# Products of a linear-attention prologue on column halves and quarters of TensorE's array

## The chip, the cores and the metric

The kernel runs on one core of a Trainium2 chip. The metric is device time in microseconds of one execution, the median of several runs. The profile is of one execution of its own, with its own time.

## The reference

A linear attention with decay and bonus (4 batches, 8 heads, 768 tokens, 48 channels a head) feeds a mixture of 8 experts over 3072 tokens of 384 channels, whose gates are balanced by eight rounds of row and column scaling. All inputs are f32.

```python
for t in range(S):                                   # attention
    kt, vt, rt = k[:, :, t], v[:, :, t], r[:, :, t]
    cur = einsum('bhd,bhe->bhde', u[None] * kt, vt)
    y[:, :, t] = einsum('bhd,bhde->bhe', rt, state + cur)
    state = w[None, :, :, None] * state + einsum('bhd,bhe->bhde', kt, vt)
x = y.transpose(0, 2, 1, 3).reshape(B * S, H * D)    # experts
P = balanced(exp(x @ w_gate - max))                  # 8 rounds
for e in range(E):
    out += P[:, e:e+1] * (maximum(x @ w1[e], 0) @ w2[e])
```

## The kernel before, in words

The kernel has two parts that follow each other. The attention fills about the first 260 us; beside it the first expert (expert 0) is started. Then the other seven experts run as 14 half-expert stages, to the end. The change touches the attention alone.

The attention takes the tokens in 24 chunks of 128 (`tt`), six to a batch (`c = tt % 6`). Within a chunk the recurrence is written as products. The eight heads are handled as four pairs (`NPAIR`); each head's 48 channels are padded to 64 (`HP`), so that a pair fills the 128 partitions. The decay is folded into tables (`rtab`, `ktab`, `wbd`). All operands of these products are f32, and the trace shows each such product as two instructions on TensorE (two passes), each with a weight load of its own.

For each chunk there are these steps, each one a function:

- `prep` (line 488): r and k times their tables, `rp` on GpSimdE and `kp` on VectorE.
- `bonus_dot`, `bonus` (494, 503): the term with u, `rk`, mostly on GpSimdE.
- `stage_b` (513): `rp` and `kp` are transposed on TensorE (tiles `prT`, `pkT`); ScalarE copies them out to `rT`, `kT`.
- `stage_c` (524): the scores, `pA` (line 536): for each pair `a` and each head `g` of it, 64 partitions of `kT` are the weights (128 columns) and 64 of `rT` are streamed (128 columns). So two heads stand on the two row halves of the array at once. VectorE copies the scores through the causal mask into `at` (538). Unless it is the last chunk of a batch, the state follows: `pu` (546), for each pair `kp` (128 weight columns, two heads) times v of both heads (96 columns). Only the blocks that belong to one head are wanted, and the table `wbd`, which is zero elsewhere, clears the other blocks: `S = (pu + S) * wbd`, the sum on VectorE (556), the product on GpSimdE (557).
- `stage_d` (560), one chunk later: y in the bank `py`: for `c > 0` four products of `rT` with `S` (570; 128 weight columns, 96 streamed), then for each head `at` times v (573; 128 weight columns, 48 streamed). VectorE adds the bonus and takes the scale for the split.
- `scale_x`, `stage_e`, `stage_f` (583 to 613): x is scaled, transposed (`px`) and split into f16 high and low parts; the gate's logits are taken from them.

TensorE's instructions keep the order of the program, and so do all other engines' (class `InOrder`, line 21). The loop at 733 sets that order by hand: in step `i` it has `prep(i + 2)`, `stage_b(i + 1)`, `stage_c(i)`, `stage_e(i - 2)`, `stage_d(i - 1)` and `stage_f(i - 3)`, and between them `work(n)`, which issues whole units of expert 0 (tiles `ph`: 9 products of 384 columns; `po`: 12 of them). `prepare()` takes one step at a time of a list `side`: splitting expert 0's weights and building sums of tokens for the later experts, on VectorE, ScalarE and GpSimdE. `STEPS` (721) says how many of these steps come ahead of and behind `stage_d` in the first loop steps.

Of the kernel before, what the change touches and what calls it, by code (L numbers as in the profile page):

```python
# [8 lines left out]
F32 = mybir.dt.float32  # L9
# [3 lines left out]
ALU = mybir.AluOpType  # L13
# [19 lines left out]
def rwkv_sinkhorn_moe(  # L33
# [13 lines left out]
    V, S_, G, T, Q = (  # L47
        InOrder(tc, e) for e in (nc.vector, nc.scalar, nc.gpsimd, nc.tensor, nc.sync)
    )

    B, H, S, D = r.shape
    NT, DM = out.shape
    E, _, F = w1.shape
    P = 128
    C = 128
    NPAIR = H // 2
# [7 lines left out]
    HP = 64  # L64
# [63 lines left out]
    def pow2_scale(m, inv, s, down):  # L128
        V.tensor_scalar(inv, m, 1e-30, down, op0=ALU.max, op1=ALU.mult)
        V.tensor_single_scalar(  # L130
            inv.bitcast(I32), inv.bitcast(I32), EXP_MASK, op=ALU.bitwise_and
        )
        V.reciprocal(s, inv)
# [135 lines left out]
    ac = att.enter_context(tc.tile_pool(name="ac", bufs=1))  # L269
    ld = att.enter_context(tc.tile_pool(name="ld", bufs=3))  # L270
    at2 = att.enter_context(tc.tile_pool(name="at2", bufs=2))
    ps3 = att.enter_context(tc.tile_pool(name="ps3", bufs=4, space=PSUM))
# [69 lines left out]
    def fill(x_):  # L342
        n = x_.shape[1]
        S_.mul(
            x_.rearrange("p (a q) -> p a q", q=HP),
            unit[:, :1, 1:].broadcast_to([P, n // HP, HP]), 0.0,
        )
# [3 lines left out]
    wbd = ac.tile([P, NPAIR, 2, D], F32, name="wbd")  # L351
# [10 lines left out]
    rp_ = [ac.tile([P, H, HP], F32, name=f"rp{i}") for i in range(2)]  # L362
    kp_ = [ac.tile([P, H, HP], F32, name=f"kp{i}") for i in range(3)]
    at_ = [ac.tile([P, H, C], F32, name=f"at{i}") for i in range(2)]
    for t_ in rp_ + kp_:
        G.memset(t_[:, :, D:], 0.0)
    fill(at_[0].rearrange("p h c -> p (h c)"))

    rk0 = at2.tile([P, H, D], F32, tag="rk", name="rk_0", bufs=3)
# [91 lines left out]
    for j in range(2):  # L461
        rows = slice(j * HP, j * HP + D)
# [61 lines left out]
    def stage_c(tt):  # L524
        d = st[tt]
        c = tt % NCHB
        rT, kT = d["rT"], d["kT"]
        at = at_[tt % 2].rearrange("p (a g) c -> p g a c", g=2)
        pas = []
        for g in range(2):  # L530
            pa = ps3.tile([P, NPAIR, C], F32, tag="pa", name=f"pA_{tt}_{g}")
            pas.append(pa)
        for a in range(NPAIR):
            for g in range(2):
                rows = slice(g * HP, g * HP + HP)
                T.matmul(pas[g][:, a, :], kT[rows, a, :], rT[rows, a, :], start=True, stop=True)
        for g in range(2):
            V.copy_predicated(
                at[:, g], maski.unsqueeze(1).broadcast_to([P, NPAIR, C]), pas[g]
            )  # L540
        if c < NCHB - 1:
            vn = loads[tt]["v"]
            kp = kp_[tt % 3].rearrange("p (a j) d -> p a (j d)", j=2)
            pu = ps3.tile([P, NPAIR, 2 * D], F32, tag="pa", name=f"pu_{tt}")
            for p_ in range(NPAIR):
                T.matmul(
                    pu[:, p_, :], kp[:, p_, :],
                    vn[:, 2 * p_ : 2 * p_ + 2, :].rearrange("p j d -> p (j d)"),
                    start=True, stop=True,
                )  # L550
            sn = at2.tile([P, NPAIR, 2 * D], F32, tag="S", name=f"S_{tt}", bufs=3)
            wb = wbd.rearrange("p a j d -> p a (j d)")
            if c == 0:
                V.tensor_tensor(sn, pu, wb, op=ALU.mult)
            else:
                V.tensor_tensor(sn, pu, d["S"], op=ALU.add)
                G.tensor_tensor(sn, sn, wb, op=ALU.mult)
            st.setdefault(("S", tt + 1), sn)

    def stage_d(tt):  # L560
        d = st[tt]
        c = tt % NCHB
        vn = loads[tt]["v"]
        at = at_[tt % 2]
        py = ps3.tile([P, H, D], F32, tag="pa", name=f"py_{tt}")
        pyp = py.rearrange("p (a j) d -> p a (j d)", j=2)
        first = True
        if c > 0:
            for p_ in range(NPAIR):
                T.matmul(pyp[:, p_, :], d["rT"][:, p_, :], d["S"][:, p_, :], start=first, stop=False)  # L570
                first = False
        for h in range(H):
            T.matmul(py[:, h, :], at[:, h, :], vn[:, h, :], start=first, stop=(h == H - 1))
            first = False
        x = at2.tile([P, DM], F32, tag="x", name=f"x_{tt}")
        V.tensor_tensor(x, py.rearrange("p h d -> p (h d)"), d["av"].rearrange("p h d -> p (h d)"), op=ALU.add)
        m = at2.tile([P, 1], F32, tag="xm", name=f"xm_{tt}")
        V.tensor_reduce(m, x, axis=AX.X, op=ALU.max, apply_absolute_value=True)
        s = at2.tile([P, 1], F32, tag="xs", name=f"xs_{tt}")
        pow2_scale(m, inv_s[:, tt : tt + 1], s, 0.125)  # L580
        d["x"], d["s"] = x, s
# [134 lines left out]
    for sg in range(3):  # L716
# [2 lines left out]
        side += steps  # L719

    STEPS = {
        0: (2, 1), 1: (1, 2), 2: (3, 1), 3: (1, 1),
        4: (1, 1), 5: (1, 1), 6: (2, 1), 7: (1, 1), 8: (1, 1),
    }

    def n_steps(i):
# [6 lines left out]
    for i in range(NTT + 3):  # L733
# [15 lines left out]
        if i < NTT:  # L749
            bonus(i)  # L750
            if ("S", i) in st:
                st[i]["S"] = st.pop(("S", i))
            stage_c(i)
# [17 lines left out]
        if 1 <= i <= NTT:  # L771
            stage_d(i - 1)
# [417 lines left out]
    for s in range(NS):  # L1190
        tasks = stage_tasks(s)
        for g in range(NG):
            for j in range(2):
                for n, nxt in enumerate(g1_slots(s, g, j)):
# [3 lines left out]
                    i = j * NPR + n  # L1198
# [37 lines left out]
```

## Time and profile before

| what | us |
|---|---|
| median of 3 runs (1562.79 to 1563.94) | 1563.07 |
| the profiled execution's own time | 1562.66 |
| its span in the profile | 1561.0 |
| TensorE busy | 1550.4 |
| VectorE busy | 1021.1 |
| ScalarE busy | 673.6 |
| GpSimdE busy | 581.8 |

The profile comes from the hardware's records of one execution. PE is TensorE's products, PEld its weight loads, DVE VectorE, ACT ScalarE, POOL GpSimdE, SP the queue that issues most DMAs. A group row has the engine, the operation, the tile written and those read, the shape, the count, then the busy time in us and the mean of one in ns, then the idle time of the engine ahead of it and who ended it. `64*128` ahead of the shapes of a product is rows times columns of the array that it uses. Products overlap in the pipeline, so the mean of one is its latency, and not the distance to the next; that is read from the chain of waits, which follows the work that ended last back from the end and gives for each piece its start, its length and its count. Line numbers are of little help, since a helper (line 29) issues nearly all instructions: one goes by tiles.

### The profile page before, as it was taken

To read this page: it belongs to the slowest core of one execution; us is meant where nothing else is said; L and a number is where in the kernel's file an instruction comes from. 1 tells how busy PE (TensorE), PEld (TensorE's weight loads), DVE (VectorE), ACT (ScalarE), POOL (GpSimd) and SP (SyncE) were. 2 spreads that over 40 slices of the span, in tenths; PEclk is the share of its full clock that TensorE was granted. 3 is DMA by queue.
4 is the path that set the end of the run, shared out by engine and by line. 5 is a ranking of instruction groups with operands and counts; after the bars stand their busy time and mean duration, and the time that the engine had idled before them with its cause. 6 is when DMAs were issued, how large, how long until landed. Compare 5 with 4: busy or idle time off the path is not lost.

```text
span 1561.0 us, 24064 instructions
## 1 busy us (share of the span) xinstructions
PE 1550.4 (99%) x9297; PEld 898.9 (58%) x9297; DVE 1021.1 (65%) x1694; ACT 673.6 (43%) x1192; POOL 581.8 (37%) x686
## 2 busy tenths in 40 slices
PE   8999999999999999999999999999999999999999
PEld 6878776655555555555555555555555555555555
DVE  8876674957666676666676666666666656656554
ACT  4334333534444354544444454544444444535320
POOL 7767764620012424243342424342423324242200
PEclk9999999999999999999999999999999999999999
DMA  9333311221215657576766676665555555556433
GB/s 198 68 87 81 80 51 42 93 79 45 97 60 105 76 86 115 84 127 89 128 87 119 85 127 90 95 96 68 86 57 99 58 94 61 96 59 97 56 91 132
DMA packets 167638, 138.26 MB, mean 89 GB/s; under 512 B 90337, under 2 KB 161762, under 8 KB 167522
## 3 DMA queue, kind: packets, MB, share of 16 engines
q0 software_dynamic: 44928, 61.36, 33.0%
q1 hardware_dynamic: 122384, 75.35, 17.2%
q8 instruction: 73, 1.20, 0.3%
q14 instruction: 43, 0.35, 0.1%
q10 hardware_dynamic: 210, 0.00, 0.0%
HBM read 55.39 MB, written 80.23 MB: 87 GB/s over the span
## 4 chain that ended last, share of the span: by engine, by line
PE 95%; DVE 3%; POOL 0%; issue 0%; ACT 0%; POOLq 0%; DVEq 0%; ACTq 0%
PE po L29 47%; PE bZ L29 11%; PE bY L29 11%; PE ph L29 5%; PE bA L29 5%; PE bB L29 5%; PE py L29 3%; PE bC L29 2%; PE pA L29 1%; PE pu L29 1%; PE px L29 1%; PE prT L29 1%; PE pkT L29 0%; DVE ws L29 0%; POOL rk L29 0%
## 5 line engine op out<-in xcount | busy, mean ns | idle before, releaser
L29 PE MATMUL po<-ws,hbx 128*128 128x384 f16 x3360 | 736.8, 326 | 0.0
L29 POOL DMA_DIRECT2D accd<-stg x288 | 249.7, 867 | 695.8 <-ACT stg L29 677.4
L29 PEld LDWEIGHTS <-hbx 128*128 128x128 f16 x3504 | 336.3, 98 | 292.4 <-issue 0.9
L29 PEld LDWEIGHTS <-ws 128*128 128x128 f16 x3096 | 302.5, 98 | 243.9 <-issue 1.4
L29 ACT ACTIVATE hbx<-tb 128x512 f16<-128x512 f32 x224 | 141.0, 630 | 450.4 <-DVE tb L29 450.4
L29 PE MATMUL po<-ws,hb 128*128 128x384 f16 x1248 | 323.0, 326 | 0.8 <-DVE ws L29 0.8
L29 DVE TENSOR_TENSOR tb<-bY,tb 128x512 f32<-128x512 f32 x168 | 116.2, 692 | 195.7 <-PE bY L29 195.5
L29 ACT ACTIVATE stg<-po,pe 128x384 f32<-128x384 f32 x312 | 179.1, 574 | 121.7 <-PE po L29 96.0
L29 PE MATMUL bZ<-xv,ws 128*128 128x512 f16 x840 | 227.0, 379 | 0.4 <-DVE tb L29 0.4
L29 PE MATMUL bY<-xv,ws 128*128 128x512 f16 x840 | 227.0, 379 | 0.0
L29 DVE TENSOR_TENSOR tb<-bZ,tb 128x512 f32<-128x512 f32 x168 | 115.6, 688 | 136.0 <-PE bZ L29 136.0
L29 PEld LDWEIGHTS <-hb 128*128 128x128 f16 x1248 | 121.8, 98 | 93.9 <-issue 1.0
L29 POOL TENSOR_TENSOR ucb<-rawb 128x256 f32<-128x256 f32 x84 | 76.2, 957 | 117.9 <-DMA rawb<-in_moe_w_dram 117.9
L29 DVE TENSOR_TENSOR tb<-bB,tb 128x512 f32<-128x512 f32 x112 | 77.5, 692 | 48.8 <-PE bB L29 46.9
L29 PE MATMUL ph<-hbx,ws 128*128 128x384 f16 x576 | 104.2, 326 | 0.5 <-DVE hb L29 0.5
L29 DVE SCALAR_TENSOR_TENSOR hb<-tb,hbx 128x512 f16<-128x512 f32 x112 | 77.3, 690 | 24.6 <-ACT hbx L29 19.5
L29 PE MATMUL bA<-xv,ws 128*128 128x512 f16 x336 | 90.8, 379 | 0.0
L29 PE MATMUL bB<-xv,ws 128*128 128x512 f16 x336 | 90.8, 379 | 0.0
L29 DVE SCALAR_TENSOR_TENSOR hbx<-tb,hbx 128x512 f16<-128x512 f32 x112 | 78.0, 696 | 14.7 <-ACT hbx L29 10.4
L29 DVE SCALAR_TENSOR_TENSOR hb<-ph,hb 128x384 f16<-128x384 f32 x64 | 35.4, 554 | 43.5 <-ACT hb L29 43.1
L29 ACT COPY tb<-bZ 128x512 f32<-128x512 f32 x56 | 32.7, 585 | 65.5 <-PE bZ L29 65.5
L29 ACT ACTIVATE hb<-ph 128x384 f16<-128x384 f32 x64 | 31.1, 487 | 62.5 <-PE ph L29 61.6
(168 smaller groups left out, 1608.0 us busy)
## 6 DMA issues: line engine op xcount, KB each, us to landing
accd<-stg POOLq DMA_DIRECT2D x288, 192.0 KB, 3.6
rawb<-in_moe_w_dram SPq DMA_DIRECT2D x28, 768.0 KB, 6.8
e0d<-stg SPq DMA_DIRECT2D x48, 192.0 KB, 1.9
hb<-e0d SPq DMA_DIRECT2D x48, 192.0 KB, 3.8
vn<-in_v_dram SPq DMA_DIRECT2D x24, 192.0 KB, 2.9
accd<-stg SPq DMA_DIRECT2D x24, 192.0 KB, 1.8
accd<-hb POOLq DMA_DIRECT2D x24, 192.0 KB, 4.8
rawb<-accd SPq DMA_DIRECT2D x24, 192.0 KB, 2.4
```

The costliest lines, as they stand in the source:

```text
L29: return lambda *a, **k: self.tc.keep_in_program_order(f(*a, **k))
```

## The change

Four things are edited, all in the attention. The state's tiles `S` become three fixed ones, and their blocks that belong to no head are set to zero once at the start. The scores are issued in column halves as well as row halves, so each product has 64 rows and 64 weight columns, and the streamed 128 columns stay. The state is taken head by head: 64 weight columns of `kp`, and the 48 columns of v of that head alone, written to the head's own half of the partitions; the update of `S` is done in two half-partition operations on VectorE and two on GpSimdE. The products of y are issued for the two halves of the tokens (64 weight columns each). Three entries of `STEPS` move a preparation step of loop step 1 to loop step 0 and put one more into loop step 6.

```diff
+    ss_ = [ac.tile([P, NPAIR, 2, D], F32, name=f"S{i}") for i in range(3)]
...
+    for t_ in ss_:
+        for j in range(2):
+            G.memset(t_[j * HP : (j + 1) * HP, :, 1 - j, :], 0.0)
...
-                T.matmul(pas[g][:, a, :], kT[rows, a, :], rT[rows, a, :], start=True, stop=True)
+                for hs in (slice(0, HP), slice(HP, C)):
+                    T.matmul(pas[g][hs, a, :], kT[rows, a, hs], rT[rows, a, :], start=True, stop=True)
...
-            pu = ps3.tile([P, NPAIR, 2 * D], F32, tag="pa", name=f"pu_{tt}")
+            pu = ps3.tile([P, NPAIR, D], F32, tag="pa", name=f"pu_{tt}")
             for p_ in range(NPAIR):
-                T.matmul(
-                    pu[:, p_, :], kp[:, p_, :],
-                    vn[:, 2 * p_ : 2 * p_ + 2, :].rearrange("p j d -> p (j d)"),
-                    start=True, stop=True,
-                )
...
+                for j in range(2):
+                    T.matmul(
+                        pu[j * HP : (j + 1) * HP, p_, :], kp[:, p_, j * HP : (j + 1) * HP],
+                        vn[:, 2 * p_ + j, :], start=True, stop=True,
+                    )
+            sn = ss_[tt % 3]
+            for j in range(2):
+                rows = slice(j * HP, (j + 1) * HP)
...
+                    V.tensor_tensor(sn[rows, :, j, :], pu[rows], d["S"][rows, :, j, :], op=ALU.add)
+            if c:
+                for j in range(2):
+                    rows = slice(j * HP, (j + 1) * HP)
+                    G.tensor_tensor(
+                        sn[rows, :, j, :], sn[rows, :, j, :], wbd[rows, :, j, :], op=ALU.mult
+                    )
...
-                T.matmul(pyp[:, p_, :], d["rT"][:, p_, :], d["S"][:, p_, :], start=first, stop=False)
+                for hs in halves:
+                    T.matmul(
+                        pyp[hs, p_, :], d["rT"][:, p_, hs], d["S"][:, p_].rearrange("p j d -> p (j d)"),
+                        start=first, stop=False, skip_group_check=True,
+                    )
...
-            T.matmul(py[:, h, :], at[:, h, :], vn[:, h, :], start=first, stop=(h == H - 1))
+            for hs in halves:
+                T.matmul(
+                    py[hs, h, :], at[:, h, hs], vn[:, h, :],
+                    start=first, stop=(h == H - 1), skip_group_check=True,
+                )
...
-        0: (2, 1), 1: (1, 2), 2: (3, 1), 3: (1, 1),
-        4: (1, 1), 5: (1, 1), 6: (2, 1), 7: (1, 1), 8: (1, 1),
+        0: (2, 2), 1: (0, 2), 2: (3, 1), 3: (1, 1),
+        4: (1, 1), 5: (1, 1), 6: (2, 2), 7: (1, 1), 8: (1, 1),
```

More of the change, by code (lines that the diff above doesn't have):

```diff
@@ L543, in stage_c @@
             kp = kp_[tt % 3].rearrange("p (a j) d -> p a (j d)", j=2)
-            pu = ps3.tile([P, NPAIR, 2 * D], F32, tag="pa", name=f"pu_{tt}")
+            pu = ps3.tile([P, NPAIR, D], F32, tag="pa", name=f"pu_{tt}")
             for p_ in range(NPAIR):
-                T.matmul(
-                    pu[:, p_, :], kp[:, p_, :],
-                    vn[:, 2 * p_ : 2 * p_ + 2, :].rearrange("p j d -> p (j d)"),
-                    start=True, stop=True,
-                )
[L551 to L557, printed above, removed]
+                for j in range(2):
[6 more added lines that the diff above has]
+                rows = slice(j * HP, (j + 1) * HP)
+                if c == 0:
+                    V.tensor_tensor(sn[rows, :, j, :], pu[rows], wbd[rows, :, j, :], op=ALU.mult)
+                else:
+                    V.tensor_tensor(sn[rows, :, j, :], pu[rows], d["S"][rows, :, j, :], op=ALU.add)
[5 more added lines that the diff above has]
+                    )
             st.setdefault(("S", tt + 1), sn)
@@ L566, in stage_d @@
         pyp = py.rearrange("p (a j) d -> p a (j d)", j=2)
+        halves = [slice(i * HP, (i + 1) * HP) for i in range(2)]
         first = True
```

## The prediction

> **What bounds the kernel now.** I read the page first, then the table of busy time by stretch, then the chain of waits inside the attention, then the groups of that stretch. The page:
>
> ```profile
> span 1561.0 us, 24064 instructions
> ...
> PE 1550.4 (99%) x9297; PEld 898.9 (58%) x9297; DVE 1021.1 (65%) x1694; ACT 673.6 (43%) x1192; POOL 581.8 (37%) x686
> ...
> PE 95%; DVE 3%; POOL 0%; issue 0%; ACT 0%; POOLq 0%; DVEq 0%; ACTq 0%
> ```
>
> TensorE is 99% busy and carries 95% of the chain. A busy share tells nothing of the pace of its instructions, though, and the change touches only the attention, in the first 260 us. The table by stretch (busy us and count of PE, weight load, DVE, ACT, POOL, then granted clock, DMA share, GB/s):
>
> ```profile
> 20.00:60.00 40.00, 38.17 (x344) 31.95 (x343) 36.76 (x74) 13.85 (x25) 32.88 (x31) 1.00 0.65 137
> 60.00:100.00 40.00, 39.21 (x348) 31.90 (x346) 31.25 (x65) 15.83 (x29) 23.39 (x24) 1.00 0.30 58
> 100.00:140.00 40.00, 40.00 (x341) 31.14 (x340) 25.91 (x55) 14.49 (x29) 31.45 (x36) 1.00 0.43 101
> ...
> 220.00:260.00 40.00, 39.58 (x333) 30.38 (x331) 24.35 (x51) 10.95 (x24) 22.48 (x28) 1.00 0.07 26
> ```
>
> Until 60 us VectorE is 92% busy (36.76 of 40). From 60 us on it has room (31.25, then 24 to 26 of 40) and TensorE has none. The chain of waits from 60 to 260 us says the same:
>
> ```profile
> by line: PE ph L29 23.4%; PE py L29 22.3%; PE po L29 21.1%; PE pA L29 9.8%; PE pu L29 8.0%; PE px L29 4.2%; PE prT L29 3.7%; PE pkT L29 3.3%; DVE ws L29 1.3%; DVE xm L29 0.6%; DVE x L29 0.6%; DVE inv_s L29 0.3%; ACT xsc L29 0.3%; DVE hb L29
> ```
>
> The products that the change edits, py (y), pA (scores) and pu (state), are 40% of a 200 us chain that is nearly all TensorE. So each is worth its own length there, and about nothing before 60 us. How long each is, from the chain in order of time (start, us):
>
> ```profile
> 204.90 1.72 PE py L29 x16
> 207.68 1.46 PE ph L29 x9
> 209.14 1.09 PE pA L29 x16
> 210.24 1.06 PE pu L29 x8
> 211.30 1.95 PE po L29 x12
> ...
> 215.04 2.61 PE py L29 x24
> ...
> 241.81 1.09 PE pA L29 x16
> 242.91 2.06 PE po L29 x12
> ```
>
> Three things are to be read here.
>
> Pace: py with 24 instructions takes 2.61 us and with 16 takes 1.72, so one takes 0.89/8 = 0.111 us. The 16 pA are eight pairs, one on each half of the rows; at 0.111 a pair they would need 0.89.
>
> Change of shape: pA takes 1.09, so going from the whole array to row halves cost 1.09 - 0.89 = 0.20 us. pu, eight at 0.111, takes 1.06: going back cost 0.17. po right after pA takes 2.06 where it elsewhere takes 1.95: into an f16 product the return cost 0.11.
>
> What sets the 0.111: not the streamed columns, since py with 96 and with 48 of them and pu with 96 have the same pace. It is the weight load of 128 f32 columns. The groups from 60 to 260 us:
>
> ```profile
> L29 PE MATMUL py<-vn,at 128*128 128x48 f32 x304 | 36.3, 273 | 0.0
> L29 PE MATMUL pA<-rT,kT 64*128 64x128 f32 x288 | 20.9, 285 | 0.0
> L29 PE MATMUL pu<-vn,kp 128*128 128x96 f32 x120 | 17.0, 284 | 0.0
> L29 PE MATMUL py<-S,rT 128*128 128x96 f32 x128 | 16.5, 272 | 0.0
> ...
> L29 PEld LDWEIGHTS py<-vn,at 128*128 128x128 f32 x304 | 35.5, 192 | 0.0
> L29 PEld LDWEIGHTS px<-ident,xsc 128*128 128x128 f32 x59 | 7.6, 141 | 2.4 <-ACT xsc L29 0.8
> L29 PEld LDWEIGHTS pmax_w<-ident,wma 128*1 128x1 f32 x1 | 0.1, 84 | 0.0
> ```
>
> Each f32 product is two instructions (two passes). In this stretch there are 288/16 = 18 score blocks, 120/8 = 15 pu, 304/16 = 19 y products, of which 128/8 = 16 have the 8 state instructions.
>
> **The change, part by part.** *The pace of a half.* py and pu become pairs of instructions with 64 weight columns each, side by side in the array. Nothing in this trace loads 64 f32 columns, or works on column halves. From above: the load gets no shorter than in proportion, 0.111/2 = 0.056 us; from below: in the transposes a load of 1 column takes 84 ns and one of 128 takes 141, so 64 columns fewer are at least 57 x 64/127 = 29 ns less, and the pace 0.083. I take 0.058 (half and 2 ns), since py's own row is the nearest: its load lasts 192 ns and is the thing repeated every 111. Two other limits stay clear of it or take over:
>
> ```profile
> 217.65 0.13 PE px L29 x6
> ...
> 281.20 0.34 PE pc L29 x2
> ```
>
> The first is chain time of six load-and-multiply pairs in f16, 22 ns each, so a pair of halves can be issued in about 50 ns, and the four quarters in about 100. The second streams 192 f32 columns twice in 0.34 us, 0.88 ns a column: 96 columns need 0.085, 128 need 0.113, 48 need 0.042. So a pair of the state part of y goes at 0.085, a pair of the rest at 0.058, a pair of pu (now 48 columns, the two heads apart) at 0.058, and four quarters of the scores at 0.111 as before, because 128 columns still stream through each.
>
> *Changes of shape.* pA and pu change shape on entry already; the first load, exposed there, is half as long, so 0.20 becomes 0.15 and 0.17 becomes 0.12. New are the exit from pu (0.11, as pA to po) and y's entry (0.15) and exit (0.11). No row shows whether a change of columns alone costs anything, so each lies between 0 and 0.20; I take the prices of the row halves. The Trainium skill, "TensorEngine Tiling (Array Packing)", Key Properties, says that changing the tiling mode drains TensorE; by it the three new ones are paid, and the row-half prices above agree with it.
>
> *The sum from 60 to 260 us.*
> - Scores: 8 x 0.111 + 0.15 = 1.04 for 1.09; 18 x 0.05 = 0.9 us less.
> - State: 0.12 + 8 x 0.058 + 0.11 = 0.69 for 1.06; 15 x 0.37 = 5.6 less.
> - y with state: 0.15 + 8 x 0.085 + 16 x 0.058 + 0.11 = 1.87 for 2.61; 16 x 0.74 = 11.8 less. Without: 0.15 + 16 x 0.058 + 0.11 = 1.19 for 1.72; 3 x 0.53 = 1.6 less.
>
> Together 19.9 us less on TensorE. With no price for the three new changes of shape it is 19 x 0.26 + 15 x 0.11 = 6.6 more, 26.5; at a pace of 0.083 it is 0.025 x (15 x 8 + 19 x 16) = 10.6 less, 9.3.
>
> *VectorE and GpSimdE.* The state's update is cut into two half-partition operations of 192 elements:
>
> ```profile
> L29 DVE TENSOR_TENSOR S<-pu,S 128x384 f32<-128x384 f32 x12 | 6.5, 544 | 0.0
> ...
> L29 POOL TENSOR_TENSOR ws<-ws 128x256 f32<-128x256 f32 x51 | 36.2, 725 | 1.5
> ...
> L29 POOL TENSOR_TENSOR S<-S,wbd 128x384 f32<-128x384 f32 x12 | 12.0, 996 | 1.2 <-DVE S L29 1.2
> ```
>
> On POOL 128 elements more cost 996 - 725 = 271 ns, so 192 take about 0.59 and two 1.18, +0.18 us. On VectorE two of 192 lie between the 0.544 of one of 384 and twice that; if a quarter of it is fixed time, an estimate, they take 0.68, +0.14. Fifteen times that is 2 us on VectorE and 2.2 on POOL (12 x 0.18). The reader of S is the y product of the next chunk, some 10 us later (py at 204.90 and 215.04 above), so TensorE doesn't wait for it; queued behind it on VectorE are the next steps' drains. If that cover went, it would cost 0.3 us a chunk, 5 us. Where VectorE has least room, in the 60 to 100 us stretch, TensorE's 40 us shrink by some 4 and leave 31.3 + 0.6 in 36, near the 92% at which it bounds the stretch before; I give back 2 us of the gain there.
>
> *Startup.* Six memsets of 64x192 on POOL stand ahead of rk's first product:
>
> ```profile
> 5.46 0.49 POOL L29 MEMSET kp<- 128x128 f32 x3
> 5.93 0.99 POOL L29 TENSOR_TENSOR rk<-rn,kn 128x384 f32<-128x384 f32 x1
> 12.11 2.28 POOL L29 TENSOR_TENSOR rp<-rn,rtab 128x384 f32<-128x384 f32 x2 [5.19 <-ACT rtab L29]
> ```
>
> At 0.16 to 0.3 us each (three of 128 elements take 0.49) they are 1 to 1.8 us, hidden in the 5.19 us that POOL then waits for rtab; uncovered they would cost as much. The moved STEPS bring one preparation step of chunk 1 into chunk 0, and one more into chunk 6, on the same queues in the same order: 0, at most 1 us either way. Before 60 us I count nothing for TensorE, since VectorE is the bound.
>
> Sum: -19.9 + 2 = -18 us. The profiled execution took 1562.66 us, with 1.66 around its span, and the median of the runs is 1563.07, 0.4 more. So 1563.07 - 18 = 1545 us, and for this case alone 1537 (-26.5) to 1555 (-9.3, with some of the 2 given back).
>
> **The rivals.** *Loads in turn* (slower). The halves' products overlap, but both loads come from the same rows, and weights enter one after the other: 2 x 0.058 = 0.116 a pair. Then pu is 0.12 + 8 x 0.116 + 0.11 = 1.16 (+0.10), y with state 0.15 + 24 x 0.116 + 0.11 = 3.04 (+0.43), without 2.12 (+0.40), scores 1.08. In all 1.5 + 6.9 + 1.2 - 0.2 = +9.4, 1572 us. It decides once a pair takes over 0.10, where the shape changes are no longer paid for. For it: only row halves, which read different rows, are seen side by side. Against it: the pair of row halves shows that loads of two tiles do run at once (16 in 0.89 us). 15%.
>
> *Streams in turn* (slower). The quarters that share rows also stream in turn: scores 8 x 0.226 + 0.15 = 1.96 (+0.87), 18 x 0.87 = 15.7 on top of the loads, with the 0.2 back: 1588 us. 9%.
>
> *No overlap at all* (slower). If a load in column halves can't pass the products in flight, a pair is two loads and two streams, 2 x (0.058 + 0.042) = 0.20 for y and pu, 0.286 for the state part, 2 x 0.171 = 0.34 for the scores: 16 x 3.1 + 3 x 1.7 + 15 x 0.8 + 18 x 1.8 = +99, 1662 us. The trace speaks against it for the whole array: at 0.111 an instruction, load and stream (0.042 to 0.085) of the same rows must overlap. 3%. The Trainium skill has it as a rule, "TensorE: Matmul & The Clock Gate", Packing small matmuls, row/col tiling: loads overlap products in flight only where the row group differs; the same section has column tiles running at once.
>
> *VectorE takes the gain.* If the in-order drains of 60 to 260 us already set the pace behind the busy TensorE, the stretch stays 200 us long: 1563 us. For it: 92% until 60 us; against: 24 to 26 of 40 later. 7%.
>
> **How the numbers follow.** Side by side 66%, with its own range 1537 to 1555; loads in turn 15%, streams in turn 9%, VectorE 7%, no overlap 3%. The range runs from 1537 up to 1573 so that it takes in loads in turn and VectorE too; left out are the two worse cases (12%) and the edges. A measurement of this kernel can tell some 0.2%, 3 us, from no change: faster 0.66, same 0.07, slower 0.27.
>
> **What would show it.** Right: from 60 us on, in the chain, y with state near 1.9 us, pu near 0.6, pA still near 1.05, a po or ph behind pu 0.11 longer, and the attention's last y product some 18 us earlier; 48, 16 and 32 instructions in place of 24, 8 and 16. Loads in turn: y near 3.0 and pA 1.08. Streams in turn: pA near 2. VectorE: y short, but idle time of PE with DVE as releaser. The prediction is wrong if y takes over 2.6 us, or if the attention ends earlier and the time doesn't follow.

## The result, and the profile after

The kernel after takes 1546.85 us (median of 4 runs, 1546.49 to 1547.09) against 1563.04 of the kernel before: 16.2 us less, ratio 0.9895, 95% interval [0.9878, 0.9912]. I had said 1545.

The page of the kernel after: its span, TensorE's row, and the chain by engine.

```profile
span 1544.8 us, 26300 instructions
...
PE 1524.8 (99%) x10385; PEld 865.9 (56%) x10385; DVE 1021.6 (66%) x1714; ACT 673.3 (44%) x1192; POOL 590.3 (38%) x708
...
PE 90%; DVE 4%; POOL 3%; issue 1%; ACT 1%; DMA 0%; POOLq 0%; ACTq 0%; DVEq 0%
```

TensorE has 25.6 us less to do (1550.4 before), and the span is 16.2 us shorter. So some 9 us of the work saved turned into TensorE's idle time, and the chain now runs over other engines in more places (90% on PE for 95%). Where, the table by stretch of the kernel after shows (columns as in the prediction):

```profile
20.00:60.00 40.00, 32.80 (x565) 24.89 (x564) 37.22 (x78) 14.14 (x25) 34.17 (x36) 1.00 0.63 135
60.00:100.00 40.00, 38.95 (x603) 29.47 (x603) 35.99 (x79) 17.30 (x32) 24.95 (x26) 1.00 0.38 80
100.00:140.00 40.00, 38.97 (x546) 28.59 (x545) 29.07 (x62) 16.08 (x31) 37.17 (x43) 1.00 0.41 92
```

From 20 to 60 us TensorE is busy 32.8 us instead of 38.2, and VectorE sets the time as before (37.2). There the shorter products gain nothing. From 60 us on TensorE is nearly full again.

The chain in order of time of the kernel after (start, us, what); the first row stands right behind the pu of the chunk before, the others are one chunk:

```profile
199.78 2.06 PE po L29 x12
...
208.47 1.03 PE pA L29 x32
209.50 0.60 PE pu L29 x16
...
213.13 0.33 PE px L29 x3
213.46 1.73 PE py L29 x48
215.19 0.24 PE px L29 x6
```

Twice as many instructions take less time: y 1.73 us (48 of them) for 2.61, pu 0.60 (16) for 1.06, pA 1.03 (32) for 1.09. The price of the new changes of shape stands behind them: the px that follows y takes 0.24 for 0.13, the po that follows pu 2.06 for 1.95, 0.11 each.

The weight loads of the same stretch:

```profile
L29 PEld LDWEIGHTS py<-vn,at 128*64 128x64 f32 x608 | 19.7, 138 | 0.5 <-issue 0.5
L29 PEld LDWEIGHTS pA<-rT,kT 64*64 64x64 f32 x576 | 15.5, 133 | 5.7 <-issue 5.7
```

A load of 64 columns takes 138 ns where 128 took 192: 54 less, which is half of the 111 ns at which the whole loads followed each other, and not the 29 that the transposes would have given.

What TensorE waited for between the seventh scores and the end of the attention: first the kernel before, then the kernel after.

```profile
PE po L29 <- DVE ws L29: 0.8, 1, 0.8
PE px L29 <- ACT xsc L29: 0.4, 1, 0.4
```

```profile
PE px L29 <- DVE hbx L29: 4.4, 7, 1.3
PE pmax_w L29 <- DVE md_w L29: 0.4, 1, 0.4
```

TensorE reached the gate's product seven times before VectorE had its operand (hbx) ready, 4.4 us in all (3.2 us in a second profile of the same kernel, `after_again` below).

### The profile page after: what moved, and what is told of

It reads as the page before. It is cut to its first block, busy times and chain, and to the rows that moved or that the text cites. A ratio compares the mean times of both kernels' runs of the same rounds, so it can differ in the third digit from the quotient of the medians.

```text
span 1544.8 us, 26300 instructions
## 1 busy us (share of the span) xinstructions
PE 1524.8 (99%) x10385; PEld 865.9 (56%) x10385; DVE 1021.6 (66%) x1714; ACT 673.3 (44%) x1192; POOL 590.3 (38%) x708
## 4 chain that ended last, share of the span: by engine, by line
PE 90%; DVE 4%; POOL 3%; issue 1%; ACT 1%; DMA 0%; POOLq 0%; ACTq 0%; DVEq 0%
PE po L29 47%; PE bZ L29 12%; PE bY L29 12%; PE bA L29 5%; PE bB L29 5%; PE ph L29 4%; PE bC L29 2%; POOL rk L29 2%; PE py L29 1%; PE pA L29 1%; DVE ws L29 0%; PE px L29 0%; POOL ws L29 0%; POOL rp L29 0%; DVE hbx L29 0%
## 5 line engine op out<-in xcount | busy, mean ns | idle before, releaser
L29 ACT COPY tb<-bZ 128x512 f32<-128x512 f32 x56 | 32.8, 585 | 65.5 <-PE bZ L29 65.5
```

The costliest lines, as they stand in the source:

```text
L29: return lambda *a, **k: self.tc.keep_in_program_order(f(*a, **k))
```

## The experiments

The theory: two column halves load and stream side by side, so a pair costs one half load; the gain is TensorE's from 60 us on, less what VectorE and GpSimdE take back. The main rival: 64 columns are cheap in themselves, whatever stands beside them. Each run has runs of the kernel before beside it on its chip (medians 1562.8 to 1563.3).

### Side by side, or only smaller?

**y in turn.** All of the left half of the tokens first, then all of the right.

```diff
-            for p_ in range(NPAIR):
-                for hs in halves:
+        for hs in halves:
+            for p_ in range(NPAIR):
                     T.matmul(pyp[hs, p_, :], d["rT"][:, p_, hs], ...)
...
-        for h in range(H):
-            for hs in halves:
+            for h in range(H):
                 T.matmul(py[hs, h, :], at[:, h, hs], ...)
```

> The kernel after, with the same 48 instructions of y issued in another order: all of the left half of the tokens first, then all of the right half, so that neighbouring instructions use the same columns. Side by side (my theory: a pair costs one load only because its two members use different columns): 16 x 0.082 + 32 x 0.058 + 0.25 = 3.4 us for y instead of 1.73, 19 x 1.6 = about +30 us, near 1577. Rival (a load of 64 columns is simply cheap, or the queue puts the instructions side by side by itself, whatever the order): y stays at 1.73 and the time at 1547.

Measured 1567.1 us, ratio to before 1.0027 [1.0016, 1.0037]. The chain of that kernel:

```profile
207.67 1.80 PE py L29 x32
217.59 3.12 PE py L29 x47
```

y takes 3.12 us with state and 1.80 without (32 instructions, 0.056 us each: in turn, one half takes as long as a pair does side by side; 47 stands for 48, since one record is missing). The same instructions, of the same shape, make the kernel 20 us slower than the kernel after and 4 us slower than the one before. So the gain of y is the standing side by side, and the queue doesn't bring it about by itself. I had expected +30: y pays 16 x 1.39 + 3 x 0.7 = 24 us, and the kernel gets back TensorE's waits on hbx, of which this one has 0.3 us in its first 300 us, against 7.2 in the kernel after.

**Four quarters of the tokens in y.** The halves are replaced by four slices of 32 (`halves = [slice(i * 32, (i + 1) * 32) for i in range(4)]`).

> The kernel after, with y issued for four quarters of the tokens (32 weight columns each, four instructions side by side, 96 in all). A load of 32 columns is about 0.029 us and streams stay 0.042 and 0.082. My theory: issue bounds it, four load-and-multiply pairs at 22 to 25 ns each are 0.09 to 0.10 us: 8 x 0.10 + 16 x 0.10 + 0.2 = 2.6 us for y instead of 1.73, 19 x 0.85 = +16 us, 1563. Rival (the load goes on setting the pace): 8 x 0.082 + 16 x 0.042 + 0.2 = 1.5 us, -4 us, 1543.

Measured 1544.97 us, against 1546.84 of the kernel after measured beside it. Chain and weight loads of that kernel:

```profile
212.34 0.33 PE px L29 x3
212.66 1.48 PE py L29 x96
214.14 0.24 PE px L29 x6
```

```profile
L29 PEld LDWEIGHTS py<-vn,at 128*32 128x32 f32 x1216 | 15.2, 110 | 0.5 <-issue 0.5
L29 PEld LDWEIGHTS py<-S,rT 128*32 128x32 f32 x512 | 10.4, 109 | 2.7 <-issue 2.5 <-PE px L29 0.2
```

96 instructions in 1.48 us, 15 ns each. The rival is right and my bound of issue is wrong: the 22 ns a pair of load and product that I had read off px were the pace of one stream of f16 instructions into the whole array; side by side they go faster. Loads fall by another 28 ns (138 to 110), and now the streams account for the time, 8 x 0.082 + 16 x 0.042 + 0.15 = 1.48 us. That it isn't a faster bound of issue, the two parts of y show: in the timeline the 32 state products, with 96 columns, take 0.69 us until the next part starts (212.59 to 213.28), 22 ns each, and the 64 others, with 48 columns, 0.79 until px (214.07), 12 ns each; issue would treat both alike. The time falls by 1.9 us of the 19 x 0.25 = 4.8 on TensorE; TensorE's waits on hbx grow (9.0 us in the first 300 us, against 7.2 and 6.2 in the two profiles of the kernel after).

### Each part alone

**Scores on row halves again**, the rest as after (the first line of the scores' diff undone).

> The kernel after, with the scores on row halves again (16 instructions in place of 32). My theory: 128 streamed columns set the pace of the scores either way, so only the exposed first load comes back: pA 1.09 instead of 1.03 us, 18 x 0.06 = +1 us, 1548. Rival (the quarters carry a real part of the gain): pA nearer 1.5 us, +5 us or more.

Measured 1547.58 us (1547.04 to 1548.47), 0.7 more than the kernel after, which is hardly more than the spread. Its chain decides:

```profile
209.30 1.09 PE pA L29 x16
210.39 0.60 PE pu L29 x16
```

As expected: the quarters save 0.06 us a chunk, the half load that is exposed on entry. The 128 streamed columns keep the pace at 0.11.

**y by token halves alone**, on the kernel before.

> The kernel before, with y alone on token halves. By the lengths in the profile after: y with state 1.73 instead of 2.61 us (16 times), without 1.2 instead of 1.72 (3 times), the px behind it 0.11 longer (19 times): -15.6 + 2.1 = -13.5 us. No memsets, no split update of S, so the first 60 us take as long as before. With 1 to 2 us lost to waits: 1550 to 1551. Rival (the loss until 60 us comes from shorter y, which meets VectorE's waits earlier): chunk 6 late all the same, 1551 to 1552.

Measured 1549.71 us, ratio 0.9915 [0.9902, 0.9929]: 13.3 us less, the bulk of the gain.

**The state by heads alone**, on the kernel before, with the fixed S, the memsets and the split update.

> The kernel before, with the state by heads alone (fixed S tiles, memsets, split update), y and scores and STEPS as before. pu 0.60 instead of 1.06 us, the next product 0.11 longer: 15 x 0.35 = -5.3 us on TensorE. My theory: the split update (0.72 for 0.54 us on VectorE, 1.25 for 1.0 on GpSimdE) and the memsets are what costs the 1.5 us until 60 us: chunk 6 about 1.5 us late, 1559. Rival (the split costs nothing): 1557.5.

Measured 1559.88 us, ratio 0.9980 [0.9971, 0.9989]: 3.2 us less, of 5.3 on TensorE. The parts alone give 13.3 + 3.2 + some 0.7 (scores) = 17.2 us; together they give 16.2.

### What takes part of it back

The start of the seventh scores says how late the stretch is that VectorE bounds. From there to the first product into `bA`, with which the stage behind the attention starts, it is TensorE's stretch. From the timelines, in us:

| kernel | first scores | seventh scores | from there to bA | time |
|---|---|---|---|---|
| before | 14.98 | 61.07 | 273.31 | 1563.04 |
| y alone | 15.98 | 60.74 | 260.38 | 1549.71 |
| state alone | 16.69 | 62.43 | 268.05 | 1559.88 |
| after | 16.69 | 62.53 | 255.58 | 1546.85 |
| after, again | 16.69 | 63.71 | 255.64 | 1546.84 |
| memsets later | 15.14 | 64.33 | 255.58 | 1547.75 |
| one update | 15.93 | 61.58 | 254.25 | 1544.14 |

**The kernel after once more**, to see how far one profile stands for a kernel.

> The kernel after once more, unchanged, for the spread of a profile: the time 1546.9 within 0.5 us; the start of the first scores (16.69 us) and of the seventh (62.53) within 0.5 us if these stand for the kernel, 1 us or more apart if they are chance.

The time is the same; the first scores too; the seventh are 1.2 us apart, and the stretch behind them is the same within 0.1 us. So a difference of 1 us at the seventh scores isn't read from one profile, and the verdicts below go by the times. Taken together the profiles do say something: of all kernels here, nine with the update of S split in two start the seventh scores at 62.14 to 64.33 us, and the four with a whole update at 60.74 to 61.58 (a tenth with the split, pu beside y below, has a loss of its own and starts them at 65.59).

**The memsets later**: the loop with the six memsets of S stands behind rk's first product.

> The kernel after, with the six memsets of S behind the first product of rk on GpSimdE, where it then waits for rtab anyway. My theory: the first scores come 1.7 us late (16.69 against 14.98) because the memsets push that product beside VectorE's work (its operation on good took 0.90 instead of 0.14 us) and TensorE's pause grows; so the first scores come near 15.0 again, and 1 to 1.5 us of it reaches the end: 1545.5. Rival (the stretch until 60 us has slack for it): the first scores come early, the time stays at 1547.

1547.75 us (1546.86 to 1548.55), no gain. The mechanism at the start is there. The operation on good in VectorE's timeline, first of the kernel after, then of this one:

```profile
8.15 0.90 DVE L29 TENSOR_TENSOR good<-wt,wsafe 128x4 f32<-128x4 f32 x1
```

```profile
8.23 0.14 DVE L29 TENSOR_TENSOR good<-wt,wsafe 128x4 f32<-128x4 f32 x1
```

It is short again, and the first scores come 1.55 us earlier; nothing of it reaches the seventh. My theory fell: the stretch has slack for the memsets. Of the 1.55 us, about 1.0 isn't the memsets' either. In the kernel after, TensorE stands still for 2.98 us before the tables' transposes (`pt_tab`), and its granted clock is 0.50 from 12 to 15 us. In the kernel with the old STEPS (next), with the memsets early and 0.90 us on good all the same, it stands still for 1.87 us, the clock stays at 1.00, and the first scores start at 15.69. y alone, which has no memsets, stands still for 2.75 us, has 0.50 from 11 to 14 us, and starts them at 15.98.

**The old STEPS**, the rest as after.

> The kernel after, with the STEPS of the kernel before. I counted the move at nothing, within 1 us: 1546 to 1548. Rival (in the stretch until 60 us, which VectorE bounds, the order of its steps decides): 2 us or more either way, seen in the start of the seventh scores (62.5 us after, 61.1 before).

1546.39 us (1545.15 to 1546.72): no difference that can be told.

**One update of S per engine**, as before the change; pu is broadcast to both heads' blocks and the product with wbd clears those that belong to no head. The memsets of S, no longer needed, go too.

```diff
-            for j in range(2):
-                rows = slice(j * HP, (j + 1) * HP)
...
+            both = pu.unsqueeze(2).broadcast_to([P, NPAIR, 2, D])
+            V.tensor_tensor(s4, both, d["S"], op=ALU.add)
+            G.tensor_tensor(sn, sn, wbd.rearrange("p a j d -> p a (j d)"), op=ALU.mult)
```

> The kernel after, with the update of S in one operation per engine again: VectorE adds pu, broadcast to both heads' blocks, to all of S (384 elements), GpSimdE multiplies by wbd, which clears the blocks of no head; the memsets are not needed. My theory: the split update is what costs the stretch until 60 us its 1.4 us (state_only has it, y_only does not): the seventh scores start near 61.0 instead of 62.5 and the time falls by 1 to 2 us, to 1545. Rival (the loss is in the memsets or in chance): seventh scores at 62.5, 1546.5.

1544.14 us (1543.97 to 1544.20), 2.7 us less than the kernel after measured beside it (1546.83 to 1547.86). The update's groups, kernel after and this one, then what TensorE waits for in this one from 60 us on:

```profile
L29 DVE TENSOR_TENSOR S<-pu,S 64x192 f32<-64x192 f32 x24 | 8.3, 347 | 0.4
...
L29 POOL TENSOR_TENSOR S<-S,wbd 64x192 f32<-64x192 f32 x24 | 14.1, 588 | 0.9
```

```profile
L29 DVE TENSOR_TENSOR S<-pu,S 128x384 f32<-128x384 f32 x12 | 6.5, 545 | 0.0
...
L29 POOL TENSOR_TENSOR S<-S,wbd 128x384 f32<-128x384 f32 x12 | 12.0, 1002 | 0.0
```

```profile
PE px L29 <- DVE hbx L29: 2.1, 6, 0.9
```

Two halves cost 0.69 us on VectorE for 0.55, and 1.18 on GpSimdE for 1.00. In the kernel after no engine waits for S; but what stands behind it in those queues comes later, and TensorE waits less for hbx once the update is whole (2.1 us, against 4.4 and 3.2 in the two profiles of the kernel after). By the table about half of the 2.7 us is gained from the seventh scores on (254.25 for 255.6) and the rest before them. The run takes out the memsets together with the split, and none takes them out alone; since with the memsets later GpSimdE reaches rp at 12.27 us, nearly as in the kernel before (12.11), and the time doesn't fall, the 2.7 us are put down to the split update.

From the seventh scores on, the split update is not enough to make TensorE wait: with the state alone that stretch gets 5.3 us shorter, all that TensorE saves there, and TensorE waits 0 us for hbx in it. y alone loses 1.0 us there (12.9 shorter, of 13.9 saved), with 0.4 us of waits for hbx. With both, in the kernel after, it waits 3 to 4 us: the less time TensorE takes, the less of it covers what VectorE, ScalarE and GpSimdE do for hbx.

### A change of shape less

**pu beside y.** pu and its update are moved from behind the scores to behind y, which has the same shape.

> The kernel after, with pu and the update of S moved from behind the scores to behind y, which has the same shape (all rows, column halves): one change of shape per chunk is gone. By the ends of instructions in the profile after, pA to pu costs 0.13 us over the pace of pu, pu to po 0.11; in their place stands only pA to po, 0.11. So 15 x 0.13 = -2 us, 1545. Rival (S is finished later and its updates stand elsewhere in VectorE's order): TensorE waits for VectorE, no gain or slower by 1 to 3 us.

1557.75 us, ratio 0.9966 [0.9952, 0.9979]: 11 us slower than the kernel after. Its waits from 60 to 245 us:

```profile
POOL S L29 <- DVE S L29: 29.4, 10, 4.5
DVE hbx L29 <- ACT hbx L29: 26.8, 12, 3.7
...
ACT hbx L29 <- POOL rk L29: 16.4, 6, 3.8
...
PE px L29 <- DVE hbx L29: 12.6, 6, 3.4
```

GpSimdE stands at S until VectorE has done its part, and rk behind it comes late; ScalarE can't write hbx before rk has read it, VectorE and then TensorE follow. A lower clock adds to it. Two rows of the same kernel, the stretch from 80 to 94 us and the transposes behind one such wait:

```profile
80.00:94.00 14.00, 11.19 (x160) 8.33 (x162) 11.01 (x23) 5.64 (x10) 8.95 (x9) 0.88 0.24 45
```

```profile
88.87 0.30 PE L29 MATMUL px<-wgp,hbx 128*128 128x16 f16 x6 [2.81 <-DVE hbx L29]
...
89.04 1.09 PE L29 MATMUL prT<-ident,rp 128*128 128x128 f32 x4
```

After TensorE has stood for 2.81 us the granted clock of the stretch is 0.88 (0.65 from 88 to 90 us, 0.50 from 90 to 92, then 1.00 again), and four transposes take 1.09 us that take 0.64 in the kernel after at 60.06 us. The length of a wait alone doesn't decide this: after 3.40 us, until 62.98 us, the clock stays at 1.00 in the same profile; after 1.91 us, until 183.07, it is 0.54 from 184 to 186.

**The update a step later.** pu stays beside y; the update of S is taken in the next loop step, ahead of the scores, when VectorE and GpSimdE find pu long done.

```diff
+            if i:
+                update_s(i - 1)
             if ("S", i) in st:
...
         if 1 <= i <= NTT:
             stage_d(i - 1)
+        if i < NTT:
+            stage_s(i)
```

> The kernel after, with pu beside y and the update of S taken one loop step later, ahead of the next scores. In state_beside_y the update on GpSimdE waited up to 4.25 us for VectorE's part, and behind it in GpSimdE's order stood rk, then ScalarE's and VectorE's part of hbx, then px on TensorE (12.6 us of waits). My theory: with the update where VectorE has long done its part, that chain of waits is gone and the change of shape saved shows: 1544 to 1546. Rival (the update is not the cause, but pu itself between y and px): again slower than 1550.

1542.29 us, ratio 0.9866 [0.9851, 0.9881], 4.6 less than the kernel after; so it was the place of the update. Its chain:

```profile
190.11 1.07 PE py L29 x32
...
195.31 2.06 PE po L29 x12
...
199.15 1.73 PE py L29 x48
200.88 0.47 PE pu L29 x16
201.35 0.24 PE px L29 x6
```

pu behind y takes 0.47 us, eight pairs at 0.058 and no entry: 0.13 less than behind the scores. That is 15 x 0.13 = 2 us of the 4.6; the run forecast 1 to 3. The stretch from the seventh scores to bA is 3.8 us shorter (251.8 for 255.6), and in it TensorE waits 1.6 us for hbx instead of 3.2 to 4.4, so the later update takes some waits away as well.

**Both**: the update a step later and whole.

> state_update_next with the update in one operation per engine. If both savings are independent: 1542.3 - 1.5 = 1541. If the stretch until 60 us is bound by something else: 1542.

1540.67 us, ratio to before 0.9857 [0.9840, 0.9873], 6.2 less than the kernel after measured beside it (1546.84), of the 4.6 + 2.7 = 7.3 that the two savings would add up to. It is faster than the kernel before and the kernel after.

## Why the prediction was right

Side by side was right, and the terms of the sum came out as worked: y with state 1.73 + 0.11 = 1.84 us (I had 1.87), without state 1.07 + 0.11 = 1.18 by the chain of state_update_next (1.19), pu 0.60 + 0.11 (0.58 + 0.11), pA 1.03 (1.04). With them the sum is 16 x 0.77 + 3 x 0.54 + 15 x 0.35 + 18 x 0.06 = 20.3 us; I had 19.9.

The choice of 0.058 for a pair, by the row that is nearest, was right: pu behind y takes 0.47 us, where the bound from the transposes (0.083) would make it 0.66.

The rivals of loads and streams in turn are out: y takes 1.73 us, not 3.04, and pA 1.03, not 1.96. So is no overlap at all. The Trainium skill's rule ("TensorE: Matmul & The Clock Gate", Packing small matmuls) that loads overlap products in flight only in another row group is not what these rows show: y's halves use all rows, each load takes 138 ns, and a pair goes every 58.

The changes of shape cost what the row halves had cost (0.11 on exit), also where only the columns change; the Trainium skill's drain on a mode switch ("TensorEngine Tiling (Array Packing)", Key Properties) agrees.

What was mis-sized is the part given back: 2 us, all of it to VectorE between 60 and 100 us. Between the seventh scores and bA the kernel gains 273.3 - 255.6 = 17.7 us, so 2.6 of the 20.3 are lost there, spread over the stretch. Another 1.5 us is lost before 60 us, where I had counted nothing; of that, the repeat shows, about 1 us can be chance, though the thirteen profiles above set the split update apart. So the rival "VectorE takes the gain" came true in part, for some 4 us. The profile before had a sign of it that I passed over: later than 100 us VectorE's load isn't 24 to 26 of 40 throughout, but nearly 30 in one row of the same table.

```profile
140.00:180.00 40.00, 40.00 (x349) 31.67 (x349) 29.92 (x60) 14.36 (x28) 27.60 (x29) 1.00 0.37 85
```

By one_update, 2.7 of these 4.1 us go to the split update, whose own length I had priced rightly (+0.14 and +0.18 us a chunk; +0.15 and +0.18 measured). The step that failed is "so TensorE doesn't wait for it", which looked at the reader of S alone. TensorE doesn't wait for S, but for hbx, which stands behind S in the same queues, and it does so once y is shorter too: with the state alone nothing is lost from the seventh scores on. The prediction let the cover shrink between 60 and 100 us alone; its price for a cover that went altogether, 5 us, is above what was lost. The memsets and STEPS were nothing in the time, as I said, though the memsets are not hidden where I said: they move rk beside VectorE's operation on good.

## What to carry to other kernels

Small f32 products whose pace is the weight load gain from a cut into column halves only when the two halves are neighbours in the program; in turn they cost more than the whole did. The cut pays as far as the stream is shorter than the load that is cut, so first compare the two: a whole load goes every 0.111 us, and the pair became 0.058 with 48 streamed columns, 0.082 with 96, and no shorter with 128. Count each new change of shape on entry and exit, and put products of one shape next to each other, but watch what moves with them. An operation that nobody waits for still has a price in an in-order queue: ask who waits for what stands behind it, and ask it again with all savings made, since each of them takes away cover.

## What the runs showed of the hardware

- Products on column halves that share all rows start beside each other, loads too: 48 instructions in 1.73 us, 96 on column quarters in 1.48, 15 ns each, less than the 22 ns that a pair of f16 load and product takes in the whole array (px, six in 0.13 us).
- A load of f32 weights takes 192 ns for 128 columns, 138 for 64 and 110 for 32.
- VectorE's operation on 4 elements a partition (good) takes 0.90 us (8.15 to 9.05) where GpSimdE multiplies rk at the same time (7.78 to 9.03 in that timeline), and 0.14 where it doesn't; so in all fourteen profiles, nine of the first kind and five of the second. Memsets on GpSimdE beside it (6.89 to 8.64 in the kernel with the memsets later) leave it at 0.14.
- After some pauses of TensorE its granted clock is about half for some 3 us: in the kernel after it is 0.50 from 12 to 15 us, after 2.98 us; with pu beside y 0.50 from 90 to 92, after 2.81 us, and 0.54 from 184 to 186, after 1.91. After 1.87 us (old STEPS) and once after 3.40 us (pu beside y) it stays at 1.00, so the length of the pause alone doesn't decide.
